# Forgetting attention and a gated feed-forward on one core: attention of the first two batches ahead of the load issues, score tiles paired across batches, the last project in two halves

## The chip, the cores and the metric

The kernel runs on one core of one Trainium2 chip. The metric is the time of one execution on the device, in microseconds (us); lower is better. Line numbers L… are those of the kernel before; the changed kernel's lines stand three to five further down.

## The reference

Attention with a decay, over 8 batches of 8 heads with 576 tokens and 64 values a head, then a feed-forward block with root-mean-square norm:

```python
scores = q @ k.T / 8 + (cum[i] - cum[j])        # cum = cumsum(log(clip(f)))
attn = softmax(where(j > i, -1e9, scores)); x = attn @ v          # tokens by (heads * 64)
xn = x / sqrt(mean(x * x) + 1e-6) * rms_g
out = (silu(xn @ w_gate) * (xn @ w_val)) @ w_out    # 4608 x 512 -> 1536 -> 512
```

## The kernel before

Tokens of a batch are cut into five blocks of 128 (the last has 64; `LAST` = 4). For each query block `qi` and key block, TensorE makes a score tile for all 8 heads at once in one of two `sc` tiles of PSUM (L468), ScalarE takes the exponent into one of eight `PT` tiles (L486), GpSimd zeroes the upper triangle of the diagonal tile (L493), and TensorE multiplies the tiles of a query block by `Vs` (L512), the values scaled with the decay (L443, by VectorE in the first two batches and by GpSimd later). VectorE divides by the sum (L526, L528) into `x`; ScalarE squares it (L544), GpSimd makes the root (L548, L549), ScalarE scales (L556), and the result is turned into `xT`: on TensorE for the first two groups (L564), by a transposing DMA later (L578).

The feed-forward works on nine groups of 512 tokens: one for each batch's first 512, and one (`xTr`) of the last 64 of all batches. A `gate` is a pair of matmul blocks (L623, `wg` and `wv`), a tanh on ScalarE (L635) and two products on VectorE (L637, L630) into `hT`. For group 0, and for group 1 in this setting, a gate takes 4 chunks of 128 tokens. A `project` is 12 matmuls with `wo` into one `ff` tile (L648), a copy into `ores` (L661) and a store (L665, L674). Four `ff` tiles in PSUM serve all of this. While group 0 runs, VectorE folds `rms_g` into the weights (`weigh`, L357), since group 0 takes it from `xT`.

The order on every engine comes from a planner (`Plan.run`), which runs when the program is built: each piece of work is a unit with an engine, an assumed duration, a key, units it depends on, and ring buffers it takes and gives. A clock steps through assumed times; an engine that is free takes the ready unit with the lowest key. What it writes down is a fixed order per engine; on the chip each engine works through its own list and waits at the head of it. `SEEDS` shift a few keys at random before this. Loads are units of the queue that issues them (SP, or GpSimd, which has the casting loads of q, k, v and the weights), with keys from -20 to -9.25 for batch 0 and the weights; the attention of the first two batches has keys from -9 upwards. Later batches have keys by group.

In the last project the 512 columns of one `ff` tile are copied in two halves, by ScalarE and by VectorE, and stored by SP and ScalarE, 64 rows each.

Of the kernel before, what the change touches and what calls it, by code (L numbers as in the profile page):

```python
# [13 lines left out]
ACT = mybir.ActivationFunctionType  # L14
# [2 lines left out]


XPE, DT1, WIDE1 = 2, 0, 0
SEEDS = (84657, 89789, 467802, 542893, 578548, 39129, 244901, 271533, 218637, 949787, 548179, 128631, 931054,  # L20
         308866, 728294, 159527, 419945, 172881, 127940, 429679, 253611, 69364, 46042, 834979, 30072, 763446,
         468225, 737993, 973909, 205828, 651373, 635195, 93425, 157523, 690164, 692741, 943081, 404019, 832688)


class Unit:
# [14 lines left out]
class Plan:  # L40
# [114 lines left out]
def fox_ffn_kernel(ctx, tc, q, k, v, f, moe_w_gate, moe_w_val, moe_w_out, moe_rms_g, out):  # L155
    nc = tc.nc
    B, H, S, D = q.shape
# [56 lines left out]
    def pe(dur, key, emit, deps=(), take=(), give=()):  # L214
        return P.add("PE", dur, key, emit, deps, take, give, lat=0.2)
# [179 lines left out]
    def turn(b, j, key):  # L395
        p0, n = rows(j)
        for dst, nm in ((T_QT, "q"), (T_KT, "k")):
            def emit(dst=dst, nm=nm):
                nc.sync.dma_start_transpose(out=dst[hold_QT[b].slot][:, :, p0:p0 + n],
                                            in_=T_qk[hold_qk[b, nm, j].slot][0:n, :])  # L400
            turned[b, nm, j] = load("SP", 1.3, (16 * n, 0.00029), key, emit, [qkload[b, nm, j]],
                                    take=[hold_QT[b]], give=[hold_qk[b, nm, j]], late=1.8)

    def turn_pe(b, j, two, key):
# [130 lines left out]
    def norm(b, js, key):  # L535

        n = rows(js[0])[1]
        sq, ms, rs = (s[0:n, b, js[0]:js[-1] + 1] for s in stat)
        us = []
        for i, j in enumerate(js):  # L540
            hx = hold_x[b, j]

            def emit(i=i, hx=hx):
                nc.scalar.activation(junk[0:n, :], T_x[hx.slot][0:n, :], ACT.Square, accum_out=sq[:, i:i + 1])  # L544
            us.append(act(0.73, key, emit, [evac[b, j, 0], evac[b, j, 1]]))

        def emit():
            nc.gpsimd.tensor_scalar(ms, in0=sq, scalar1=1.0 / DM, op0=ALU.mult, scalar2=1e-6, op1=ALU.add)  # L548
            nc.gpsimd.tensor_tensor(rs, ms, mhalf[0:n, 0:len(js)], ALU.pow)  # L549
        r = pool(0.9, key, emit, us + [iden_f])  # L550
        for i, j in enumerate(js):
            hx, hn = hold_x[b, j], Hold("xn", 1)
            g, c = (b, j * 128) if j < LAST else (B, b * 64)

            def emit(i=i, n=n, hx=hx, hn=hn):
                nc.scalar.mul(T_xn[hn.slot][0:n, :], T_x[hx.slot][0:n, :], rs[:, i:i + 1])  # L556
            u = act(0.72, key - 0.02, emit, [r], take=[hn], give=[hx])
            if g < XPE:
                hf = Hold("ff", 1)

                def tr(hn=hn, hf=hf):
                    tp = T_ff[hf.slot].bitcast(BF16)
                    for dc in range(NDC):
                        nc.tensor.transpose(tp[:, dc * 128:(dc + 1) * 128], T_xn[hn.slot][:, dc * 128:(dc + 1) * 128],  # L564
                                            ident)
                t = pe(0.25, key, tr, [u, iden], take=[hf], give=[hn])

                def cp(hf=hf, g=g, c=c):
                    tp = T_ff[hf.slot].bitcast(BF16)[:, 0:512].rearrange("p (c t) -> p c t", t=128)
                    to = T_of[g][hold_xT[g].slot][:, :, c:c + 128]  # L570
                    if g == 0:
                        nc.vector.tensor_tensor(to, tp, bcast(rgT, 128), ALU.mult)
                    else:
                        nc.vector.tensor_copy(to, tp)
                pieces[b, j] = dve(0.69 if g == 0 else 0.42, key - 0.02, cp, [t, c_rg], take=[hold_xT[g]], give=[hf])
            else:
                def tr(n=n, hn=hn, g=g, c=c):
                    nc.sync.dma_start_transpose(out=T_of[g][hold_xT[g].slot][:, :, c:c + n],  # L578
                                                in_=T_xn[hn.slot][0:n, :])
                pieces[b, j] = load("SP", 1.3, (16 * n, 0.00029), key, tr, [u], take=[hold_xT[g]], give=[hn])  # L580


    order = [(b, qi) for b in range(2) for qi in range(LAST)] + [(0, LAST), (1, LAST)]
# [2 lines left out]

    def qkey(b, qi, ahead=0.0):
        if b < 2:
            return (2 * b - 9 + 0.2 * (START[qi] + ahead)) if qi < LAST else 0.3 + 0.6 * b + 0.04 * ahead
        return akey(b, (START[qi] + ahead) / 13)  # L590

    todo = []
    for b, qi in order:
        if b >= 2 or qi == LAST or (b == 1 and qi >= 4 - 2 * DT1):
            turn(b, qi, qkey(b, qi) - 0.25)
        elif (b, qi) in {(0, 0), (0, 1), (0, 3), (1, 0), (1, 2)}:
            turn_pe(b, qi, (b, qi) in {(0, 1), (1, 0), (1, 2)}, qkey(b, qi) - 0.25)
# [12 lines left out]

    hold_hT = [Hold("hT", 4) for _ in range(G)]
# [28 lines left out]
        return dve(0.69, key - 0.1, last, [a, uv], take=[hold_hT[g]], give=[ha, hv])  # L640

    def project(g, j, key):
        hf, ho = Hold("ff", 1), Hold("ores", 1)
        last = None
        for part in range(3):
            def emit(part=part):
                for fc in range(part * 4, part * 4 + 4):
                    nc.tensor.matmul(T_ff[hf.slot], lhsT=T_hT[hold_hT[g].slot][:, fc, j * 128:(j + 1) * 128],  # L648
                                     rhs=wo[:, fc, :], start=(fc == 0), stop=(fc == NFC - 1))
            deps = [last] if part else []  # L650
            deps += hdone[g, j, part]
            deps += Lo[part // 2:part // 2 + 1 + part % 2]
            last = pe(0.865, key + 0.0001 * part, emit, deps, take=[hf] if part == 0 else [],
                      give=[hold_hT[g]] if part == 2 else [])
        end = g == B and j == 3
        halves = (slice(0, 256), slice(256, 512)) if end else (slice(0, 512),)
        hf.n = len(halves)
        cs = []
        for add, copy, cols in zip((act, dve), (nc.scalar.copy, nc.vector.tensor_copy), halves):
            cs.append(add(0.59 if len(halves) == 1 else 0.36, key - 0.05,  # L660
                          lambda copy=copy, cols=cols: copy(T_ores[ho.slot][:, cols], T_ff[hf.slot][:, cols]),  # L661
                          [last], take=[ho], give=[hf]))
        if g < B:
            t0 = g * S + j * 128
            load("SP", 0.4, (128, 0.0055), key, lambda: nc.sync.dma_start(out=out[t0:t0 + 128, :], in_=T_ores[ho.slot]), cs,  # L665
                 give=[ho])
            return
        ho.n = 2
        for i in range(2):
            eng, queue = ("ACT", nc.scalar) if end and i else ("SP", nc.sync)  # L670

            def st(i=i, queue=queue):
                t0 = (2 * j + i) * S + LAST * 128
                queue.dma_start(out=out[t0:t0 + 64, :], in_=T_ores[ho.slot][i * 64:(i + 1) * 64, :])  # L674
            load(eng, 0.4, (64, 0.0055), key, st, cs, give=[ho])
# [65 lines left out]
```

## Time and profile before

| | us |
|---|---|
| median of 3 runs | 386.04 |
| lowest and highest | 382.62, 386.28 |
| the profiled execution | 384.47 |
| its span, first to last instruction | 382.6 |

In the profile PE is TensorE's matmuls and PEld its weight loads, DVE is VectorE, ACT ScalarE, POOL GpSimd, SP SyncE; SPq, ACTq and POOLq are their queues, where DMAs are issued. A row of a timeline has its start, its length, the engine, the line, the operation with output and input tiles, a count, and in brackets how long the engine had been idle and what ended that. A row of the stretches has, for each engine, busy time and instructions in the stretch.

### The profile page before, as it was taken

How to read it: one execution, taken by the hardware profiler on the slowest of the kernel's cores; microseconds unless marked ns; L12 is line 12 of the kernel's file. 1: busy time of each engine (PE TensorE's matmuls, PEld its weight loads, DVE VectorE, ACT ScalarE, POOL GpSimd, SP SyncE). 2: the span in 40 equal slices, each digit the busy share in tenths (PEclk: the TensorE clock that was granted, in tenths of full speed). 3: DMA queues.
4: the chain of work that ended last, by engine and by line, in shares of the span. 5: the costliest groups of instructions: out<-in, count | busy, mean ns of one | idle time of the engine just before them, and what ended most of it. 6: DMA issues, size and time to landing. Idle time of an engine off the chain costs nothing.

```text
span 382.6 us, 9657 instructions
## 1 busy us (share of the span) xinstructions
PE 357.8 (94%) x3896; PEld 214.3 (56%) x3942; DVE 219.4 (57%) x458; ACT 237.5 (62%) x378; POOL 201.0 (53%) x280
## 2 busy tenths in 40 slices
PE   1799898989998999999999999999999999999994
PEld 1589875779964555555555555555555544444441
DVE  5567999556654647455655465545654645555430
ACT  5685637978988656947695669656966442332321
POOL 8975699499998665975497549841302000000000
PEclk9999999999999999999999999999999999999999
DMA  9999999979999999994999789972120210100004
GB/s 141 200 217 204 217 171 153 159 176 151 135 127 162 133 124 152 165 150 81 132 154 174 88 114 160 178 97 56 36 57 29 55 34 29 55 25 32 28 29 110
DMA packets 128869, 44.84 MB, mean 117 GB/s; under 512 B 117300, under 2 KB 121912, under 8 KB 128824
## 3 DMA queue, kind: packets, MB, share of 16 engines
q0 software_dynamic: 76368, 23.34, 61.8%
q1 hardware_dynamic: 52376, 20.74, 29.1%
q8 instruction: 31, 0.51, 0.6%
q10 hardware_dynamic: 80, 0.13, 0.2%
q14 instruction: 14, 0.11, 0.1%
HBM read 37.90 MB, written 9.44 MB: 124 GB/s over the span
## 4 chain that ended last, share of the span: by engine, by line
PE 73%; POOL 8%; DVE 7%; DMA 6%; issue 3%; ACT 1%; POOLq 0%; ACTq 0%; DVEq 0%
PE ff L623 40%; PE ff L648 22%; PE ff L512 6%; PE sc L468 5%; DMA wv<-in_moe_w_val_dram 3%; DMA xT<-xn 3%; POOL qk L315 2%; POOL Vs L443 2%; DVE hT L630 1%; POOL v L338 1%; DVE wv L357 1%; DVE ga L637 1%; ACT xn L556 1%; DVE Vs L443 1%; POOL PT L493 1%
## 5 line engine op out<-in xcount | busy, mean ns | idle before, releaser
L637 DVE SCALAR_TENSOR_TENSOR ga<-th,ff 128x512 f32<-128x512 f32 x108 | 73.4, 684 | 81.7 <-ACT th L635 80.4
L635 ACT ACTIVATE th<-ff 128x512 f32<-128x512 f32 x108 | 63.8, 595 | 75.2 <-PE ff L623 58.8
L648 PE MATMUL ff<-wo,hT 128*128 128x512 bf16 x410 | 104.9, 379 | 1.1 <-DVE x L528 0.2
L486 ACT ACTIVATE PT<-sc 128x1024 bf16<-128x1024 f32 x96 | 94.8, 1016 | 11.6 <-PE sc L468 11.5
L623 PE MATMUL ff<-xT,wg 128*128 128x128 bf16 (+1 forms) x658 | 96.1, 286 | 3.9 <-DMA xT<-xn 1.7
L623 PE MATMUL ff<-xT,wv 128*128 128x128 bf16 (+1 forms) x663 | 97.1, 286 | 2.4 <-DVE hT L630 1.7
L630 DVE SCALAR_TENSOR_TENSOR hT<-ga,ff 128x512 bf16<-128x512 f32 x108 | 73.0, 685 | 21.8 <-PE ff L623 18.7
L623 PEld LDWEIGHTS <-wg 128*128 128x128 bf16 x720 | 53.6, 98 | 39.2 <-issue 3.3
L623 PEld LDWEIGHTS <-wv 128*128 128x128 bf16 x720 | 53.2, 98 | 37.9 <-issue 2.6
L648 PEld LDWEIGHTS <-hT 128*128 128x128 bf16 x432 | 40.6, 98 | 46.4 <-issue 0.5
L493 POOL TENSOR_SCALAR_AFFINE_SELECT PT<-PT 128x1024 bf16<-128x1024 bf16 x32 | 35.3, 1104 | 48.3 <-ACT PT L486 48.3
L512 PEld LDWEIGHTS <-PT 128*128 128x128 bf16 x896 | 38.4, 99 | 15.0 <-POOL PT L493 2.3
L512 PE MATMUL ff<-Vs,PT 128*128 128x65 bf16 x896 | 43.5, 197 | 1.7 <-POOL PT L493 1.5
L443 POOL TENSOR_TENSOR Vs<-v,decT 128x512 bf16<-128x512 f32 (+1 forms) x30 | 31.5, 1049 | 17.3 <-DMA v<-in_v_dram 16.2
L661 ACT COPY ores<-ff 128x512 f32<-128x512 f32 (+1 forms) x36 | 20.8, 578 | 27.6 <-PE ff L648 27.6
L338 POOL DMA_DIRECT2D v<-in_v_dram x39 | 35.6, 915 | 3.4 <-DMA v<-in_v_dram 2.0
L468 PE MATMUL sc<-QT,KT 64*128 64x128 bf16 (+1 forms) x960 | 34.3, 214 | 1.6 <-ACT PT L486 1.3
L528 DVE TENSOR_TENSOR x<-ff,rden 128x256 f32<-128x256 f32 (+1 forms) x80 | 33.8, 423 | 2.8
L526 DVE RECIPROCAL rden<-ff 128x4 f32<-128x4 f32 (+1 forms) x80 | 14.1, 177 | 33.7 <-PE ff L512 33.5
L468 PEld LDWEIGHTS <-KT 64*128 64x128 bf16 x960 | 24.9, 97 | 13.7 <-issue 10.8
L556 ACT ACTIVATE xn<-x,rs 128x512 bf16<-128x512 f32 (+1 forms) x40 | 27.3, 716 | 7.0 <-POOL rs L549 4.4
L315 POOL DMA_DIRECT2D qk<-in_q_dram x34 | 30.0, 886 | 1.2 <-POOLq L725 0.8
(63 smaller groups left out, 218.0 us busy)
## 6 DMA issues: line engine op xcount, KB each, us to landing
out_dram<-ores SPq DMA_DIRECT2D x32, 256.0 KB, 2.4
v<-in_v_dram POOLq DMA_DIRECT2D x31, 256.0 KB, 6.3
qk<-in_q_dram POOLq DMA_DIRECT2D x26, 128.0 KB, 4.8
qk<-in_k_dram POOLq DMA_DIRECT2D x26, 128.0 KB, 6.2
wv<-in_moe_w_val_dram POOLq DMA_DIRECT2D x3, 512.0 KB, 13.2
wg<-in_moe_w_gate_dram POOLq DMA_DIRECT2D x3, 512.0 KB, 11.5
wo<-in_moe_w_out_dram POOLq DMA_DIRECT2D x2, 768.0 KB, 16.4
v<-in_v_dram POOLq DMA_DIRECT2D x8, 128.0 KB, 6.7
```

What stands on the lines that cost most here:

```text
L315: nc.gpsimd.dma_start(out=T_qk[h.slot][0:n, :].rearrange("p (h d) -> p h d", d=D), in_=src[b, :, p0:p0 + n, :].rearrange("h p d -> p h d"))
L338: queue.dma_start(out=T_v32[h.slot][0:n, :, :], in_=v[b, :, p0:p0 + n, :].rearrange("h p d -> p h d"))
L443: eng.tensor_tensor(T_Vs[hv.slot][0:n, j, :, 0:D], T_v32[h.slot][0:n, :, :], bcast(dj, D), ALU.mult)
L468: nc.tensor.matmul(t[:, par, c:c + n], lhsT=kt[r, p, kj * 128:(kj + 1) * 128], rhs=qt[r, p, qi * 128:qi * 128 + n], start=True, stop=True)
L486: nc.scalar.activation(T_of_p[hp.slot][:, 0:2 * half].rearrange("p (a c) -> p a c", a=2)[:, :, 0:cols], T_sc[h.slot][:, :, 0:cols], ACT.Ex ...
L493: nc.gpsimd.affine_select(out=d, in_=d, pattern=[[0, 8], [1, n]], compare_op=ALU.is_ge, fill=0.0, base=0, channel_multiplier=-1)
L512: nc.tensor.matmul(po[:, p, :], lhsT=T_of_p[h.slot][:, c:c + 128], rhs=vs[:, kj, 2 * p + par, :], start=(kj == 0), stop=(kj == qi))
L623: nc.tensor.matmul(T_ff[h.slot][:, c:c + n], lhsT=w[:, dc, fc * 128:(fc + 1) * 128], rhs=xT[:, dc, t0:t0 + n], start=(dc == 0), stop=(dc = ...
L630: nc.vector.scalar_tensor_tensor(hT, in0=three[0], scalar=0.5, in1=three[1], op0=ALU.mult, op1=ALU.mult)
L635: th = act(0.6, key - 0.1, lambda: nc.scalar.activation(T_th[ht.slot], T_ff[hg.slot], ACT.Tanh, scale=0.5), [ug], take=[ht])
L637: a = dve(0.69, key - 0.1, lambda: nc.vector.scalar_tensor_tensor(T_ga[ha.slot], in0=T_th[ht.slot], scalar=1.0, in1=T_ff[hg.slot], op0=ALU ...
L648: nc.tensor.matmul(T_ff[hf.slot], lhsT=T_hT[hold_hT[g].slot][:, fc, j * 128:(j + 1) * 128], rhs=wo[:, fc, :], start=(fc == 0), stop=(fc == ...
```

## The change

Five things change in the code.

1. The attention of batches 0 and 1 gets keys from -18.8 (`BASE`) instead of -9, so it goes ahead of the weights' and later loads where an engine has both (GpSimd above all: masks and roots against load issues). Their values and norms follow their scores more closely (`VA` = 1 and `NA` = 1.2 instead of 2.5 and 3.5).
2. Score tiles are issued in pairs; the odd tile at the end of a batch, which stood alone, is now paired with the first tile of the next batch.
3. The last project makes its two halves of 256 columns one after the other, each with an `ff` and an `ores` tile of its own; both are copied by ScalarE, and there are four stores of 64 rows by 256 columns (three on SP, one on ScalarE) instead of two of 64 rows by 512.
4. The planner assumes a longer transposing DMA.
5. `SEEDS` are others.

```diff
-XPE, DT1, WIDE1 = 2, 0, 0
-SEEDS = (84657, 89789, 467802, 542893, 578548, 39129, 244901, 271533, 218637, 949787, 548179, 128631, 931054,
...
+BASE = -18.8
+VA, NA = 1, 1.2
+SEEDS = (579458, 693525, 233519, 938766, 177064, 479178, 872084, 34928, 716154, 894218, 4117, 601621, 491026,
...
-            turned[b, nm, j] = load("SP", 1.3, (16 * n, 0.00029), key, emit, [qkload[b, nm, j]],
+            turned[b, nm, j] = load("SP", 1.3, (16 * n, 0.00044), key, emit, [qkload[b, nm, j]],
...
-            return (2 * b - 9 + 0.2 * (START[qi] + ahead)) if qi < LAST else 0.3 + 0.6 * b + 0.04 * ahead
+            return (2 * b + BASE + 0.2 * (START[qi] + ahead)) if qi < LAST else 0.3 + 0.6 * b + 0.04 * ahead
...
-            if len(todo) == 2 or (b == 0 and kjs[-1] == qi) or kjs[-1] == LAST:
+            if len(todo) == 2 or (b == 0 and kjs[-1] == qi) or (b, kjs[-1]) == (B - 1, LAST):
...
-        values(b, qi, qkey(b, qi, qi + 2.5))
+        values(b, qi, qkey(b, qi, qi + (VA if b < 2 else 2.5)))
...
-            norm(b, js, qkey(b, js[-1], js[-1] + 3.5))
+            norm(b, js, qkey(b, js[-1], js[-1] + (NA if b < 2 else 3.5)))
...
+        ho, cs = [Hold("ores", 1) for _ in halves], []
+        for half, cols in enumerate(halves):
+            hf, last = Hold("ff", 1), None
+            for part in range(3):
...
+                        nc.tensor.matmul(T_ff[hf.slot][:, cols], lhsT=T_hT[hold_hT[g].slot][:, fc, j * 128:(j + 1) * 128],
+                                         rhs=wo[:, fc, cols], start=(fc == 0), stop=(fc == NFC - 1))
...
+            cs.append(act(0.36 if end else 0.59, key - 0.05, lambda hf=hf, cols=cols, half=half: nc.scalar.copy(
+                T_ores[ho[half].slot][:, cols], T_ff[hf.slot][:, cols]), [last], take=[ho[half]], give=[hf]))
...
+                eng, queue = ("ACT", nc.scalar) if half and i else ("SP", nc.sync)
...
+                    queue.dma_start(out=out[t0:t0 + 64, cols], in_=T_ores[ho[half].slot][i * 64:(i + 1) * 64, cols])
```

What this does to the order is seen at three places. The first is ScalarE in the head of the program, before: `KT` is the copy of turned keys, `hT` here the decay in a buffer that is free, `PT` an exponent tile, `junk` the square of `x0`, the first query block's result, `xn0` its scaled form.

```order
L282 ACTIVATE hT1_113<-hT1_113,mid_138 64x576
L427 COPY KT0_80<-ff0_123 128x4x128
L427 COPY KT0_80<-ff1_124 128x4x2x128
L486 ACTIVATE PT0_89<-sc0_121 128x1024
L486 ACTIVATE PT1_90<-sc0_121 128x1024
L486 ACTIVATE PT2_91<-sc1_122 128x1024
L427 COPY KT0_80<-ff0_123 128x4x128
L544 ACTIVATE junk_136,sq_139<-x0_99 128x512
L486 ACTIVATE PT3_92<-sc0_121 128x1024
L486 ACTIVATE PT4_93<-sc1_122 128x1024
L486 ACTIVATE PT5_94<-sc0_121 128x1024
L556 ACTIVATE xn0_105<-x0_99,rs_141 128x512
```

The same place of the changed kernel:

```order
L430 COPY KT0_80<-ff1_124 128x4x128
L285 ACTIVATE hT1_113<-hT1_113,mid_138 64x576
L489 ACTIVATE PT0_89<-sc0_121 128x1024
L430 COPY KT0_80<-ff1_124 128x4x2x128
L547 ACTIVATE junk_136,sq_139<-x0_99 128x512
L489 ACTIVATE PT1_90<-sc1_122 128x1024
L489 ACTIVATE PT2_91<-sc0_121 128x1024
L559 ACTIVATE xn0_105<-x0_99,rs_141 128x512
L489 ACTIVATE PT3_92<-sc1_122 128x1024
L489 ACTIVATE PT4_93<-sc0_121 128x1024
L489 ACTIVATE PT5_94<-sc1_122 128x1024
```

The first copy has moved ahead of the decay, the first exponent ahead of the second copy, the square of `x0` ahead of the exponents of the second query block, its scaling ahead of the third block's, and the third copy behind all of these.

The second place is VectorE while group 0 runs, before: `ga` and `hT0` are the two products of a gate, `wg` and `wv` the folding of `rms_g`, `Vs1` the scaling of batch 1's values.

```order
L637 SCALAR_TENSOR_TENSOR ga0_116<-th0_114,ff3_126 128x512
L357 TENSOR_SCALAR wg_127<-wg_127,rgT_130 128x512 x4
L443 TENSOR_TENSOR Vs1_88<-v322_85,decT_135 128x8x64
L444 CAST Vs1_88<-decT_135 128x8
L630 SCALAR_TENSOR_TENSOR hT0_112<-ga0_116,ff2_125 128x4x128
L637 SCALAR_TENSOR_TENSOR ga1_117<-th1_115,ff1_124 128x512
L357 TENSOR_SCALAR wv_128<-wv_128,rgT_130 128x512 x4
L630 SCALAR_TENSOR_TENSOR hT0_112<-ga1_117,ff3_126 128x4x128
```

The changed kernel, as many rows from the start of its list:

```order
L446 TENSOR_TENSOR Vs1_88<-v322_85,decT_135 128x8x64
L447 CAST Vs1_88<-decT_135 128x8
L430 COPY QT1_78<-ff1_124 128x4x2x128
L640 SCALAR_TENSOR_TENSOR ga1_117<-th0_114,ff0_123 128x512
L633 SCALAR_TENSOR_TENSOR hT0_112<-ga1_117,ff3_126 128x4x128
L575 TENSOR_TENSOR xT0_109<-ff0_123,rgT_130 128x4x128
L529 RECIPROCAL rden0_142<-ff3_126 128x4
L531 TENSOR_TENSOR x4_103<-ff3_126,rden0_142 128x4x64
L640 SCALAR_TENSOR_TENSOR ga1_117<-th1_115,ff1_124 128x512
```

The first results of batch 1 (`x4`) now stand between the gates of group 0, and the folding of the weights comes later in the list.

The third place is SP's list at the end, before, with the stores of the last group (two for each of its projects):

```order
L665 DMA out_0_dram<-ores1_119 128x512
L674 DMA out_0_dram<-ores2_120 64x512 x2
L674 DMA out_0_dram<-ores0_118 64x512 x2
L674 DMA out_0_dram<-ores1_119 64x512 x2
L674 DMA out_0_dram<-ores2_120 64x512
```

And changed:

```order
L666 DMA out_0_dram<-ores1_119 128x512
L676 DMA out_0_dram<-ores2_120 64x512 x2
L676 DMA out_0_dram<-ores0_118 64x512 x2
L676 DMA out_0_dram<-ores1_119 64x512 x2
L676 DMA out_0_dram<-ores2_120 64x256 x2
L676 DMA out_0_dram<-ores0_118 64x256
```

SP has two more stores behind those of the third project; one more store of the last project is on ScalarE's queue, as before.

More of the change, by code (lines that the diff above doesn't have):

```diff
@@ L19 @@
 XPE, DT1, WIDE1 = 2, 0, 0
-SEEDS = (84657, 89789, 467802, 542893, 578548, 39129, 244901, 271533, 218637, 949787, 548179, 128631, 931054,
-         308866, 728294, 159527, 419945, 172881, 127940, 429679, 253611, 69364, 46042, 834979, 30072, 763446,
-         468225, 737993, 973909, 205828, 651373, 635195, 93425, 157523, 690164, 692741, 943081, 404019, 832688)
+BASE = -18.8
+VA, NA = 1, 1.2
+SEEDS = (579458, 693525, 233519, 938766, 177064, 479178, 872084, 34928, 716154, 894218, 4117, 601621, 491026,
+         354719, 434034, 228013, 97395, 11681, 347647, 765825, 66081, 881721, 502518, 805631, 222054, 709678,
+         173299, 242848, 187611, 334030, 497482, 17147, 635799, 701044, 138540, 384064, 613012, 295955, 674079,
+         543307, 211343, 784335, 305669, 953268)
 class Unit:
@@ L579, in tr @@
                                                 in_=T_xn[hn.slot][0:n, :])
-                pieces[b, j] = load("SP", 1.3, (16 * n, 0.00029), key, tr, [u], take=[hold_xT[g]], give=[hn])
+                pieces[b, j] = load("SP", 1.3, (16 * n, 0.00044), key, tr, [u], take=[hold_xT[g]], give=[hn])
     order = [(b, qi) for b in range(2) for qi in range(LAST)] + [(0, LAST), (1, LAST)]
@@ L642, in project @@
     def project(g, j, key):
[L643 to L654, printed above, removed]
@@ L655, in project @@
         end = g == B and j == 3
         halves = (slice(0, 256), slice(256, 512)) if end else (slice(0, 512),)
[L657 to L662, printed above, removed]
+        ho, cs = [Hold("ores", 1) for _ in halves], []
@@ new lines, in project, with emit @@
+        for half, cols in enumerate(halves):
+            hf, last = Hold("ff", 1), None
+            for part in range(3):
+                def emit(part=part, hf=hf, cols=cols):
+                    for fc in range(part * 4, part * 4 + 4):
+                        nc.tensor.matmul(T_ff[hf.slot][:, cols], lhsT=T_hT[hold_hT[g].slot][:, fc, j * 128:(j + 1) * 128],
+                                         rhs=wo[:, fc, cols], start=(fc == 0), stop=(fc == NFC - 1))
+                deps = [last] if part else []
+                deps += hdone[g, j, part]
+                deps += Lo[part // 2:part // 2 + 1 + part % 2]
+                last = pe(0.865 / len(halves), key + 0.01 * half + 0.0001 * part, emit, deps,
+                          take=[hf] if part == 0 else [], give=[hold_hT[g]] if (part, cols.stop) == (2, 512) else [])
+            cs.append(act(0.36 if end else 0.59, key - 0.05, lambda hf=hf, cols=cols, half=half: nc.scalar.copy(
+                T_ores[ho[half].slot][:, cols], T_ff[hf.slot][:, cols]), [last], take=[ho[half]], give=[hf]))
@@ L663, in project, with st @@
         if g < B:
             t0 = g * S + j * 128
-            load("SP", 0.4, (128, 0.0055), key, lambda: nc.sync.dma_start(out=out[t0:t0 + 128, :], in_=T_ores[ho.slot]), cs,
-                 give=[ho])
+            load("SP", 0.4, (128, 0.0055), key, lambda: nc.sync.dma_start(out=out[t0:t0 + 128, :], in_=T_ores[ho[0].slot]),
+                 cs, give=ho)
             return
[L668 to L675, printed above, removed]
+        for half, cols in enumerate(halves):
+            ho[half].n = 2
+            for i in range(2):
+                eng, queue = ("ACT", nc.scalar) if half and i else ("SP", nc.sync)
+                def st(i=i, queue=queue, half=half, cols=cols):
+                    t0 = (2 * j + i) * S + LAST * 128
+                    queue.dma_start(out=out[t0:t0 + 64, cols], in_=T_ores[ho[half].slot][i * 64:(i + 1) * 64, cols])
+                load(eng, 0.4, (64, 0.0055 / len(halves)), key + 0.01 * half, st, [cs[half]], give=[ho[half]])
```

## The prediction

> **What bounds the kernel now.** I read the page first, then the stretches, then the waits of TensorE, and last the timeline at the head, around 40 to 82 us, and at the end. From the page, the engines' busy time:
>
> ```profile
> PE 357.8 (94%) x3896; PEld 214.3 (56%) x3942; DVE 219.4 (57%) x458; ACT 237.5 (62%) x378; POOL 201.0 (53%) x280
> ```
>
> TensorE is busy for 357.8 of 382.6 us, and nothing in the change takes a matmul away, so all that can be won lies in the 24.8 us in which it stands still. The stretches say where those are:
>
> ```profile
> 0.00:10.00 10.00, 2.13 (x25) 1.80 (x26) 4.93 (x24) 4.82 (x6) 8.80 (x17) 1.00 1.21 148
> 10.00:20.00 10.00, 7.18 (x95) 5.66 (x96) 5.94 (x16) 6.86 (x9) 9.05 (x11) 1.00 1.41 198
> ...
> 40.00:50.00 10.00, 8.98 (x167) 8.39 (x165) 10.00 (x23) 6.30 (x8) 6.97 (x9) 1.00 1.59 209
> 50.00:60.00 10.00, 9.47 (x131) 6.22 (x129) 9.93 (x23) 5.67 (x9) 9.79 (x11) 1.00 1.97 161
> ...
> 370.00:383.00 13.00, 7.63 (x35) 3.26 (x34) 0.42 (x1) 2.13 (x4) 0.00 (x0) 0.98 0.34 82
> ```
>
> The first figure behind the comma is TensorE's, then come PEld, DVE, ACT and POOL. TensorE loses 10.7 us in the first 20, 1.6 between 40 and 60, and 5.0 at the end (382.6 less 370, less 7.63). That is 17.3; the other 7.5 are spread over all the rest. Between 40 and 60 VectorE has no gap left (10.00 and 9.93). The waits of TensorE from 20 us on name the releasers:
>
> ```profile
> PE ff L623 <- DVE hT L630: 2.5, 3, 1.5
> PE ff L623 <- DMA xT<-xn: 1.7, 2, 1.3
> PE ff L512 <- POOL PT L493: 1.0, 1, 1.0
> PE ff L623 <- DVE ga L637: 0.5, 2, 0.3
> ```
>
> So the kernel is a TensorE stream with a head, a stretch where VectorE holds it back, and a tail. The change works on all three.
>
> **The head.** These rows carry the chain up to the sixth exponent:
>
> ```profile
> 6.98 0.78 ACT L282 ACTIVATE hT<-hT,mid 64x576 f32<-64x576 f32 x1 [0.27 <-DVE mid L275]
> 7.03 0.10 PEld L414 LDWEIGHTS <-qk 128*128 128x128 bf16 x1 [7.03 <-DMA qk<-in_k_dram]
> 7.74 1.01 PE L414 MATMUL ff<-ident,qk 128*128 128x128 bf16 x8 [7.74 <-DVE ident L263]
> 8.36 0.59 ACT L427 COPY KT<-ff 128x512 bf16<-128x512 bf16 x1 [0.61 <-PE ff L414]
> 10.79 1.06 PE L420 MATMUL ff<-ident,qk 128*64 128x128 bf16 x16
> 11.79 1.04 PE L468 MATMUL sc<-QT,KT 64*128 64x128 bf16 x16
> 11.90 1.31 ACT L427 COPY KT<-ff 128x1024 bf16<-128x1024 bf16 x1 [2.95 <-PE ff L420]
> 13.07 1.03 ACT L486 ACTIVATE PT<-sc 128x1024 bf16<-128x1024 f32 x1
> 14.79 1.94 ACT L486 ACTIVATE PT<-sc 128x1024 bf16<-128x1024 f32 x2 [0.70 <-PE sc L468]
> 17.75 0.63 ACT L544 ACTIVATE junk<-x 128x512 bf16<-128x512 f32 x1 [0.54 <-DVE x L528]
> 18.38 2.83 ACT L486 ACTIVATE PT<-sc 128x1024 bf16<-128x1024 f32 x3
> 21.12 0.72 ACT L556 ACTIVATE xn<-x,rs 128x512 bf16<-128x512 f32 x1
> 25.99 0.62 PE L468 MATMUL sc<-QT,KT 64*128 64x128 bf16 x16
> ...
> L528 DVE TENSOR_TENSOR x<-ff,rden 128x256 f32<-128x256 f32 (+1 forms) x80 | 33.8, 423 | 2.8
> ```
>
> In the changed order the identity is made before the second pair of load issues, so the first transposes start when their keys land, at 7.03. Their copy follows 0.62 later (8.36 less 7.74) and ends at 8.24; the first score tile, half of the 1.04, is done by 8.9. ScalarE does the decay's exponent (0.78) in the meantime, and the first exponent starts near 9.1 instead of 13.07: a lead of 4.0 us. I do not think it lasts. The keys of the second query block still need their two groups of transposes (some 1.06 each), which now stand behind the decay's transposes; I put their end at 12.4 against 11.85, and the 1.31 copy at 13.8 against 13.2. Then ScalarE's list has the square of `x0` ahead of the next exponents. For that VectorE must first make its own copy (as long as ScalarE's, to about 13.3) and then `x0` in two halves (0.42 each and a smaller reciprocal: about 1.2), so 14.5. Before, an exponent starts 0.63 behind the square's start; so the next one comes at 15.2, 0.4 later than the 14.79 of before. From there six places run on: two exponents (1.94), the scaling of `x0` (0.72), three exponents (2.83), to 20.7. Before, ScalarE has all of this and one 0.59 copy more done at 21.84 (21.12 and 0.72); with that copy the changed list is at 21.3. I give the 0.5 to handovers, since the third block's score tiles wait for one of two `sc` tiles to be read, and call the head level: 0.0, between -3.0 (three quarters of the lead kept) and +2.0 (two exponents' time lost at the square and the scaling that now stand in front of them).
>
> GpSimd's load issues of the fourth block and of most weights now stand behind the first mask, and some behind the first root, on an engine that is busy for 8.80 and 9.05 of 10 us already. I cost that at nothing, since the first gate comes only behind the sixth score tile; if that cover is gone, it falls under the +2.0.
>
> **The VectorE stretch.** Three rows of the timeline:
>
> ```profile
> 44.56 1.95 PE L623 MATMUL ff<-xT,wg 128*128 128x128 bf16 x32 [0.78 <-DVE hT L630]
> 62.84 0.47 PE L512 MATMUL ff<-Vs,PT 128*128 128x65 bf16 x10 [1.00 <-POOL PT L493]
> 81.66 1.05 PE L623 MATMUL ff<-xT,wv 128*128 128x128 bf16 x16 [1.46 <-DVE hT L630]
> ```
>
> Before, gates of group 0 follow each other and each wants two products from VectorE, while the folding and the scaling of values also sit there. Changed, batch 1's scores and values lie between them: TensorE has work that does not wait for a product. Of the 3.0 us of waits for `hT` and `ga`, the 1.5 that are not the wait at 81.66 should go; for the 1.46 at 81.66 and the mask's 1.00 I take half, since neither the order nor the trace says which wait is next there. That is 1.5 + 0.7 + 0.5, -2.7, of which I keep -2.5 as later waits will be a little longer; the ends are 0 (they only move) and -4.0 (all go). The closer values and norms (`VA`, `NA`) carry the risk here: a value block sooner behind its scores is a value block sooner at a mask; that is the second rival.
>
> **The pairs.** A block of score matmuls starts late by a little, since it follows blocks that use all rows:
>
> ```profile
> 171.72 1.03 PE L648 MATMUL ff<-wo,hT 128*128 128x512 bf16 x4
> 172.59 1.03 PE L623 MATMUL ff<-xT,wv 128*128 128x512 bf16 x4
> 173.55 0.64 PE L468 MATMUL sc<-QT,KT 64*128 64x64 bf16 x32
> ```
>
> Starts lie 0.87 apart between two blocks of four, and 0.96 ahead of the scores: 0.09 for each entry. Three pairs across batches save three entries: -0.3. The paired tile now waits for the next batch's turned keys. No row shows such a wait; the loads run far ahead, and I take nothing, with up to 1.3 (the longest wait for a transposing DMA) as the upper end.
>
> **The tail.**
>
> ```profile
> 367.16 10.52 PE L648 MATMUL ff<-wo,hT 128*128 128x512 bf16 x47
> 376.90 0.59 ACT L661 COPY ores<-ff 128x512 f32<-128x512 f32 x1 [3.77 <-PE ff L648]
> 377.76 0.37 ACT L661 COPY ores<-ff 128x256 f32<-128x256 f32 x1 [0.28 <-PE ff L648]
> 378.17 0.42 DVE L661 COPY ores<-ff 128x256 f32<-128x256 f32 x1 [10.02 <-ACT ores L661]
> 378.62 0.58 ACTq L674 DMA_DIRECT2D out_dram<-ores  x1
> ...
> 377.51 1.75 SPq L674 DMA_DIRECT2D out_dram<-ores  x3
> ...
> out_dram<-ores SPq DMA_DIRECT2D x32, 256.0 KB, 2.4
> out_dram<-ores SPq DMA_DIRECT2D x7, 128.0 KB, 2.3
> ```
>
> TensorE ends at 377.68, and VectorE's half of the copy waits for ScalarE's: the last copy ends at 378.59, the last issues at 379.20 and 379.26. Changed, TensorE does the same columns (24 matmuls of half the width), so I keep its end. The last copy then ends at 378.13, 0.46 sooner. But SP now has five stores behind the third project, whose copy ends 0.9 earlier (12 half matmuls and four more, some 1.75, lie behind it instead of 0.86), at 376.60. Five issues of 0.58 from there end at 379.5, 0.3 later than the 379.26 of before. SP's queue takes the place of the copy. A store a quarter of 256 KB lands perhaps 0.05 sooner by the two sizes above. Tail: +0.2, between -0.5 (the copy's gain whole) and +0.6. [...]
>
> **Sum.** 0.0 - 2.5 - 0.3 + 0.2 = -2.6 against the profiled execution's 384.47 (span 382.6 and 1.9 around it), that is 381.9, so 382. The profiled run lies 1.6 below the median of the three, 386.04, and 1.9 over the lowest. What a measurement can tell from no change is about 1%, 3.8 us.
>
> **Rivals.**
>
> *The head keeps its lead.* If the square of `x0` is not late (VectorE's 1.31 copy done sooner) the exponents go on from 9.1 nearly without a gap, and 3 of the 4.0 us stay, with 0.5 from faster matmuls there: 382.0 - 3.5 = 378.5. For it: ScalarE is idle for 5.2 of the first 10 us and 3.1 of the next. Against it: the second block's copies follow loads that are issued behind the identity now, and transposes behind the decay's. The score rows show a slow state that could end: 16 matmuls take 1.04 at 11.79 and 0.62 at 25.99, with the granted clock recorded as 1.00 from 10 to 20. [...] Chance 0.27.
>
> *Masks take the place of products (slower).* In batches 0 and 1 eight value blocks have a mask from GpSimd, which is busy for nine tenths of the first 20 us and most of 50 to 60 with load issues; a value block with a smaller key stands sooner at its mask. One such wait is in the profile, 1.00 at 62.84. If seven more come at 1.0 each, 382.0 + 7 = 389.0. It decides from the third on, which eats the forecast gain; five or more make it slower than before by over half a per cent. For it: the waits row of masks. Against it: values behind the gates have other work ahead of them. Chance 0.15.
>
> *VectorE stays the bound.* Its work is the same but for one copy, and part of what it loses is not order. The lengths of the foldings:
>
> ```profile
> L357 DVE TENSOR_SCALAR wg<-wg,rgT x12: 334/337/722, 41.6 to 65.0; 128x512 bf16<-128x512 bf16 x12
> L357 DVE TENSOR_SCALAR wv<-wv,rgT x12: 334/344/1555, 45.0 to 67.0; 128x512 bf16<-128x512 bf16 x12
> ```
>
> (shortest, median, longest in ns.) The longest takes 1.2 us more than the median, while GpSimd is at work beside it. If that stays, the waits only move: 384.5 - 0.3 + 0.2 = 384.4, no change. [...] Chance 0.18.
>
> **Chances and range.** The forecast has 0.40, with a range of its own from 379.5 to 384.5; a quarter of it lies below 380.6, the bound of 1%. With the first rival (0.26 of its 0.27) that makes faster 0.36; the second rival gives slower 0.15; the rest, 0.49, is no change. Lows of all terms (-3.0, -4.0, -0.3, -0.5) would give 376.7, highs (+2.0, 0, +1.0, +0.6) 388.1. The range 377 to 387 leaves out most of the second rival and a little below.
>
> **What would show it.** Right: the first exponent near 9 us and the sixth's end near 21; no wait over 0.5 of TensorE for `hT` between 40 and 60; five SP issues in a row at the end, the last 1.8 or 1.9 behind the last matmul. Wrong: the first gate on TensorE before 19 us (first rival), several waits of L512 for masks of about 1.0 (second), a VectorE stretch full for 20 us with the same waits for `hT` (third), or a loss after 120 us, for which nothing here speaks.

## The result and the profile after

| | kernel before | changed kernel |
|---|---|---|
| median of 20 runs each, us | 382.96 | 382.76 |
| lowest and highest, us | 381.74, 388.22 | 381.31, 389.49 |
| ratio to before, 95% interval | | 0.9995 (0.9974 to 1.0015) |
| the profiled execution, us | 384.47 | 382.43 |
| its span, us | 382.6 | 380.7 |

No change that can be measured. The two profiles lie 2.0 us apart, but that of before is 1.5 above its own median, so a difference between the two pages is not yet one between the kernels.

Page and waits of TensorE of the changed kernel, from 20 us on (us in total, times, longest):

```profile
PE 357.7 (94%) x3906; PEld 214.8 (56%) x3954; DVE 219.1 (58%) x457; ACT 236.8 (62%) x379; POOL 201.0 (53%) x280
...
PE ff L515 <- DVE ga L640: 1.6, 2, 1.4
PE sc L471 <- DMA KT<-qk: 0.8, 1, 0.8
PE ff L423 <- DMA qk<-in_k_dram: 0.7, 2, 0.4
PE ff L567 <- ACT xn L559: 0.6, 1, 0.6
PE ff L423 <- DMA qk<-in_q_dram: 0.5, 1, 0.5
```

The waits for `hT` (2.5 before) are gone but for 0.2. Value blocks (L515) wait for VectorE in their place, and transposes and scores for loads of q and k, which no row of before showed. The timeline has the places:

```profile
8.44 1.02 ACT L489 ACTIVATE PT<-sc 128x1024 bf16<-128x1024 f32 x1
11.76 1.30 ACT L430 COPY KT<-ff 128x1024 bf16<-128x1024 bf16 x1 [2.29 <-PE ff L423]
13.37 0.63 ACT L547 ACTIVATE junk<-x 128x512 bf16<-128x512 f32 x1 [0.31 <-DVE x L531]
...
19.40 1.02 ACT L489 ACTIVATE PT<-sc 128x1024 bf16<-128x1024 f32 x1 [0.97 <-PE sc L471]
...
19.30 1.89 PE L626 MATMUL ff<-xT,wg 128*128 128x128 bf16 x16
...
57.33 3.21 DVE L360 TENSOR_SCALAR wg<-wg,rgT 128x512 bf16<-128x512 bf16 x4
60.47 1.26 DVE L640 SCALAR_TENSOR_TENSOR ga<-th,ff 128x512 f32<-128x512 f32 x2
...
61.18 0.65 PE L515 MATMUL ff<-Vs,PT 128*128 128x65 bf16 x16 [1.38 <-DVE ga L640]
...
72.52 0.29 PE L471 MATMUL sc<-QT,KT 64*128 64x64 bf16 x8
73.58 0.40 PE L471 MATMUL sc<-QT,KT 64*128 64x128 bf16 x8 [0.77 <-DMA KT<-qk]
```

The longest wait, 1.38 at 61.18, ends with the first of VectorE's products at 60.47, which gives an `ff` tile back; ahead of it stand four foldings that took 3.21 us instead of the 1.3 that four of the shortest (0.333) would take. The 0.77 at 73.58 is the pair: the odd tile of a batch (64x64) is done, and the next batch's tile, now in the same block, waits for its keys.

The end of the program:

```profile
365.63 10.55 PE L655 MATMUL ff<-wo,hT 128*128 128x512 bf16 x59
370.76 7.41 SPq L676 DMA_DIRECT2D out_dram<-ores  x9
376.27 0.37 ACT L662 COPY ores<-ff 128x256 f32<-128x256 f32 x1 [0.89 <-PE ff L655]
376.67 0.56 ACTq L676 DMA_DIRECT2D out_dram<-ores  x1
...
out_dram<-ores SPq DMA_DIRECT2D x3, 64.0 KB, 2.0
```

TensorE ends at 376.18, SP's last issue at 378.17, 1.99 behind it (before: 379.26 less 377.68, 1.58), and the span 4.52 behind it (before: 382.6 less 377.68, 4.92).

### The profile page after: what moved, and what is told of

It reads as the page before. It is cut to its first block, busy times and chain, and to the rows that moved or that the text cites. A ratio compares the mean times of both kernels' runs of the same rounds, so it can differ in the third digit from the quotient of the medians.

```text
span 380.7 us, 9668 instructions
## 1 busy us (share of the span) xinstructions
PE 357.7 (94%) x3906; PEld 214.8 (56%) x3954; DVE 219.1 (58%) x457; ACT 236.8 (62%) x379; POOL 201.0 (53%) x280
## 4 chain that ended last, share of the span: by engine, by line
PE 76%; DMA 14%; POOL 4%; issue 2%; ACT 2%; DVE 1%; SPq 0%; ACTq 0%; POOLq 0%
PE ff L626 41%; PE ff L655 23%; PE ff L515 6%; PE sc L471 5%; DMA wo<-in_moe_w_out_dram 4%; DMA qk<-in_q_dram 4%; DMA qk<-in_k_dram 3%; DMA KT<-qk 2%; POOL qk L318 2%; POOL PT L496 1%; DMA out_dram<-ores 1%; POOL v L341 0%; ACT PT L489 0%; DVE x L531 0%; ACT junk L547 0%
## 5 line engine op out<-in xcount | busy, mean ns | idle before, releaser
L655 PE MATMUL ff<-wo,hT 128*128 128x512 bf16 (+1 forms) x423 | 106.6, 373 | 1.1 <-issue 0.2
L515 PEld LDWEIGHTS <-PT 128*128 128x128 bf16 x896 | 38.0, 98 | 16.0 <-issue 2.0
L515 PE MATMUL ff<-Vs,PT 128*128 128x65 bf16 x896 | 42.8, 195 | 2.3 <-DVE ga L640 1.6
L341 POOL DMA_DIRECT2D v<-in_v_dram x39 | 34.3, 883 | 6.2 <-DVE rden L529 3.5
L547 ACT ACTIVATE junk<-x 128x512 bf16<-128x512 f32 (+1 forms) x40 | 25.1, 627 | 8.5 <-DVE x L531 8.1
```

The costliest lines, as they stand in the source:

```text
L341: queue.dma_start(out=T_v32[h.slot][0:n, :, :], in_=v[b, :, p0:p0 + n, :].rearrange("h p d -> p h d"))
L515: nc.tensor.matmul(po[:, p, :], lhsT=T_of_p[h.slot][:, c:c + 128], rhs=vs[:, kj, 2 * p + par, :], start=(kj == 0), stop=(kj == qi))
L655: nc.tensor.matmul(T_ff[hf.slot][:, cols], lhsT=T_hT[hold_hT[g].slot][:, fc, j * 128:(j + 1) * 128], rhs=wo[:, fc, cols], start=(fc == 0), ...
```

## The experiments

All times are ratios to the kernel before, run beside each on the same chip, with 95% intervals; 0.1% is 0.38 us.

**1. The tail alone.** The kernel before with the changed `project`; everything ahead of it stands in the same order.

```diff
         halves = (slice(0, 256), slice(256, 512)) if end else (slice(0, 512),)
+        ho, cs = [Hold("ores", 1) for _ in halves], []
...
```

> The kernel before with the last project of the changed kernel (halves in banks and tiles of their own, four stores of 64 rows by 256 columns) and nothing else; all that stands ahead of it is in the same order. By the prediction's step (five issues in a row on SP's queue take the place of the copy) the end moves by +0.2 us: the last issue on SP ends 1.9 behind the last matmul instead of 1.6, and the span ends 5.1 to 5.2 behind it instead of 4.9. The rival is read from the profile after: the smaller stores land sooner than the later issue costs, so the span ends 4.5 behind the last matmul and the time falls by 0.4.

Measured: 0.9986 (0.9963 to 1.0009). Its span and the rows of its end:

```profile
core 0 of [0], span 379.4 us
...
364.32 10.55 PE L652 MATMUL ff<-wo,hT 128*128 128x512 bf16 x60
...
369.44 7.40 SPq L673 DMA_DIRECT2D out_dram<-ores  x9
```

SP ends 1.97 behind the last matmul (376.84 less 374.87), as forecast, but the span ends 4.53 behind it: 0.39 sooner than before. The time alone could not say this; the rows do, and they are those of the changed kernel. The prediction's issue was right and its landing too long.

This profile has a second use. Its order is that of before up to the last project, yet TensorE's waits differ:

```profile
PE ff L623 <- DVE hT L630: 0.8, 2, 0.6
```

The wait of 1.46 at 81.66 and that of 1.28 at 116.58, which stand in the profile of before, are not in this one. They belonged to an execution, not to the order.

**2. Is VectorE on the path?** The folding on 8 of 512 columns, the other 504 left out, in both kernels.

```diff
-                    nc.vector.tensor_scalar_mul(w[:, dc, c0:c1], w[:, dc, c0:c1], rgT[:, dc:dc + 1])
+                    nc.vector.tensor_scalar_mul(w[:, dc, c0:c0 + 8], w[:, dc, c0:c0 + 8], rgT[:, dc:dc + 1])
```

> The changed kernel with the folding of rms_g done on 8 of 512 columns of each weight chunk; the other 504 are left out (the order on every engine is the same, VectorE has some 7 us less to do between 40 and 75 us). If VectorE still bounds the stretch from 40 to 80, the 2.0 us that TensorE waits for ga go and little takes their place: 1.5 to 3 us faster. If the late loads of q and k bound it (TensorE waits 2.8 us for DMAs from 24 to 75), those waits stay or grow by what is won: less than 0.7 us faster.

> The kernel before with the folding of rms_g done on 8 of 512 columns, the other 504 left out, the order the same. Both theories have VectorE's products as the waits of before, so both expect a gain: the 3.0 us of waits for hT and ga, of which the one at 81.66 may stay: 1.5 to 3 us faster. If it is under 0.5 us, VectorE's load was not what the stretch of before hung on, and the step of the prediction that sizes this stretch fell with it.

Measured: changed kernel 0.9907 (0.9874 to 0.9939), kernel before 0.9992 (0.9960 to 1.0024). The first is what the VectorE theory says, 3.4 us below the changed kernel's own 0.9995, though VectorE lost only 3.8 us of work there (11.7 us for 24 foldings, then 7.9; the forecast had some 7). The second is a miss for both theories: VectorE lost 5.1 us of work (11.3, then 6.2) and no time came of it. So the old order kept the foldings off the path, and the new one puts them on it. What each costs, shortest, median and longest in ns, in the changed kernel as it is (first pair) and the sums and means with 8 columns (second pair):

```profile
L360 DVE TENSOR_SCALAR wg<-wg,rgT x12: 333/340/2101, 46.3 to 70.7; 128x512 bf16<-128x512 bf16 x12
L360 DVE TENSOR_SCALAR wv<-wv,rgT x12: 333/341/1279, 63.9 to 74.0; 128x512 bf16<-128x512 bf16 x12
```

```profile
L360 DVE TENSOR_SCALAR wg<-wg,rgT 128x8 bf16<-128x8 bf16 x12 | 4.4, 433 | 0.0
L360 DVE TENSOR_SCALAR wv<-wv,rgT 128x8 bf16<-128x8 bf16 x12 | 3.5, 423 | 0.0
```

Cut to a 64th of the columns, a folding still takes 0.43 us on average, and in the kernel before one of these lasts 1.99 (the shortest 0.21): the long ones are not long from their own work.

**3. Are the late loads on the path?** The changed kernel with a sixth of the output weights loaded.

```diff
-                    out=wo[:, i * 6:(i + 1) * 6, :],
-                    in_=moe_w_out[i * 768:(i + 1) * 768, :].rearrange("(c p) f -> p c f", p=128))
+                    out=wo[:, i * 6:i * 6 + 1, :],
+                    in_=moe_w_out[i * 768:i * 768 + 128, :].rearrange("(c p) f -> p c f", p=128))
...
-                                         rhs=wo[:, fc, cols], start=(fc == 0), stop=(fc == NFC - 1))
+                                         rhs=wo[:, fc // 6 * 6, cols], start=(fc == 0), stop=(fc == NFC - 1))
```

> The changed kernel with a sixth of the output weights loaded: each of the two loads brings 128 rows of 768, and the project uses these rows six times (the other rows are left out; the order on every engine is the same, the DMA engines move 2.6 MB less between 32 and 50 us). If late loads of q and k bound the stretch from 24 to 75, TensorE's 2.8 us of waits for DMAs shrink to under 1 and the time falls by 1.5 to 2.5 us. If VectorE bounds it, the waits move to ga and hT and the time stays within 0.7 us.

Measured: 0.9970 (0.9929 to 1.0010). The waits of its TensorE:

```profile
PE ff L515 <- DVE ga L640: 3.0, 2, 1.8
...
PE ff L423 <- DMA qk<-in_k_dram: 0.9, 1, 0.9
```

This lies between the two forecasts (1.5 to 2.5 us, or within 0.7). Some 1 us may come from the lighter load, but the interval holds no gain too. The waits for DMAs fell from 2.7 us in the rows of the changed kernel to 1.9, and the wait for `ga` grew from 1.6 to 3.0: its longest, 1.8, is the one at 61.18, here at 59.24. So the loads bound at most a smaller part of the stretch.

**4. Put the foldings elsewhere.** If they are in the way between 46 and 75, move them: behind group 1's gates in VectorE's list (group 1 then takes `rms_g` from its `xT`, like group 0), or to ScalarE. In the first diff `fold` holds the six foldings and `prod` a gate's two products.

```diff
-                    if g == 0:
+                    if g < 2:
                         nc.vector.tensor_tensor(to, tp, bcast(rgT, 128), ALU.mult)
...
+        order = [u for u in P.run() if u not in fold.values()]
+        for (nm, i), u in fold.items():
+            at = max(order.index(p[nm == "v"]) for g in range(2) for p in prod[g, i])
+            order.insert(at + 1, u)
```

> The changed kernel with the six foldings of rms_g moved in VectorE's list behind the last gates of group 1 that read the same chunk (some 85 to 115 us, where VectorE is busy half the time); group 1's four copies of the turned xn multiply by rms_g as group 0's do (0.69 us planned instead of 0.42). All else stands in the same order. If in the new order the foldings lie on TensorE's path between 40 and 75, as the 3.2 us between the kernel with 8 columns and the changed kernel's own median of 20 runs say, moving them gives most of that back: 1.5 to 3 us faster than the kernel before. If leaving them out only helped because VectorE had less work in all, the waits appear again between 85 and 120 and the time stays within 0.7 us of the kernel before.

> The same move of the foldings in the kernel before, with its own order otherwise. Without the foldings that kernel was 0.3 us faster, inside the interval. If its stretch hangs on something other than the foldings (loads, the head), the move gives nothing: within 1 us of the kernel before. If the result with 8 columns was an accident of the runs, this gains 1.5 us or more like the changed kernel.

Measured: 1.0108 (1.0058 to 1.0157) and 1.0217 (1.0172 to 1.0261). Both theories miss: it is slower in both orders. The profile of the first is of its slowest execution, 3.4 us above the median of six. The changed kernel with late foldings, VectorE first, then GpSimd at the same time, then the value block that waited:

```profile
96.94 5.90 DVE L360 TENSOR_SCALAR wv<-wv,rgT 128x512 bf16<-128x512 bf16 x4
...
97.47 1.11 POOL L497 TENSOR_SCALAR_AFFINE_SELECT PT<-PT 128x1024 bf16<-128x1024 bf16 x1
98.53 1.05 POOL L447 TENSOR_TENSOR Vs<-v,decT 128x512 bf16<-128x512 f32 x1
...
101.63 1.06 POOL L447 TENSOR_TENSOR Vs<-v,decT 64x512 bf16<-64x512 f32 x1
...
103.45 1.04 PE L516 MATMUL ff<-Vs,PT 128*128 128x65 bf16 x16 [3.59 <-DVE x L532]
...
L360 DVE TENSOR_SCALAR wv<-wv,rgT x12: 334/691/3943, 82.8 to 117.5; 128x512 bf16<-128x512 bf16 x12
```

GpSimd computes without a gap from 97.47 to 102.9, and VectorE's four foldings end with it; one of them took 3.94 us instead of 0.33. GpSimd's own operations keep their 1.05. In the kernel before, with late foldings too, VectorE is busy for 9.86 of the 10 us from 95 to 105 and GpSimd for 4.99 of the first 5, and a value block that waits for VectorE comes 3.27 late, at 103.28. So the place with a half idle VectorE is a bad one. GpSimd, which is not idle there, may be the reason; no run took its work away. How much of the loss is group 1's longer copies was not separated.

On ScalarE, at the same places of the plan:

```diff
-                    nc.vector.tensor_scalar_mul(w[:, dc, c0:c1], w[:, dc, c0:c1], rgT[:, dc:dc + 1])
+                    (nc.scalar.mul if w is wv else nc.vector.tensor_scalar_mul)(
+                        w[:, dc, c0:c1], w[:, dc, c0:c1], rgT[:, dc:dc + 1])
```

> The changed kernel with the 12 foldings of the value weights (wv) done by ScalarE at the same places of the plan; those of wg stay on VectorE, the order is otherwise the same. VectorE loses 5.6 us of 11.7 (mean 527 ns each, against a shortest of 333), ScalarE gets 12 at some 0.5 us between 62 and 76, where it is busy 13.2 of 20 us. If VectorE's foldings are on TensorE's path in the new order, and longer beside GpSimd's work: 0.8 to 2.5 us faster than the changed kernel. If ScalarE's tanh and exponents become late instead: no change or up to 2 us slower.

> The changed kernel with all 24 foldings done by ScalarE, at the same places. VectorE loses 11.7 us between 46 and 75; ScalarE gets some 12 us there and would be busy about 38 of 40 us from 40 to 80. If VectorE is the bound and ScalarE has room: 2 to 3 us faster than the changed kernel, like the one with 8 columns. If ScalarE takes VectorE's place: TensorE's waits read th, xn and PT of ScalarE, and the time is 0 to 3 us over the changed kernel.

Measured: 1.0098 (1.0062 to 1.0135) and 1.0248 (1.0215 to 1.0281). Both are slower than the forecasts allowed (up to 2 and up to 3 us over the changed kernel; measured 3.9 and 9.7). ScalarE needs 0.71 us for one on average, and 0.72 with all of them there. In that kernel it is busy for 39.5 of the 40 us from 40 to 80. VectorE's waits from 40 to 82 us and a piece of the chain that ended last (start, length, work) read:

```profile
DVE ga L640 <- ACT th L638: 17.9, 5, 6.5
...
58.47 2.45 ACT wg L360 x4
61.43 0.70 DVE ga L640
62.17 0.64 PE ff L515 x16
```

VectorE has time now and waits 17.9 us for tanh, which stands behind the foldings in ScalarE's list: the bound has moved one engine on, as the rival had it, at over three times its highest price. No version tried here beats the kernels and computes the same.

**5. What the edits are worth without shifts.** `SEEDS` empty in both kernels; then the kernel before without shifts with the new keys of attention (-18.8), and with the closer values and norms too.

```diff
-SEEDS = (84657, 89789, 467802, ...
+SEEDS = ()
...
-            return (2 * b - 9 + 0.2 * (START[qi] + ahead)) if qi < LAST else 0.3 + 0.6 * b + 0.04 * ahead
+            return (2 * b - 18.8 + 0.2 * (START[qi] + ahead)) if qi < LAST else 0.3 + 0.6 * b + 0.04 * ahead
```

> The kernel before with its table of random shifts empty: the planner's keys alone set the order. If the shifts matter, 1 to 4 us slower than the kernel before; if they are noise, within 1 us.

> The changed kernel with its table of random shifts empty. Beside the kernel before without shifts it shows what the new keys, pairs and tail are worth without tuning. If attention ahead of the loads is good in itself, it is 1 to 3 us under that kernel; if the new shifts repair what the new keys do, it is 1 us or more over it; if both are noise, within 1 us.

> The kernel before without shifts (389.31 us) with one number changed: the attention of the first two batches gets the changed kernel's keys (-18.8 for -9), so that it goes ahead of load issues; values, norms, pairs and the last project are as before. In the kernel before without shifts TensorE waits 5.4 us for GpSimd's masks, which stand behind load issues; in the changed kernel without shifts (385.26) no such wait is left. If the keys do that by themselves: 3 to 4 us faster than without, some 385.5 to 386.5, with mask waits under 1.5 us. If the closer values and norms, the pairs and the tail bring it: within 1 us of 389.3.

> As the kernel with the keys of attention alone, and the values and norms of the first two batches set closer too (1 and 1.2 for 2.5 and 3.5). What is left to the changed kernel without shifts are the pairs, the last project and one planner constant. If pairs and tail are worth what the prediction's lower ends say (0.3 and 0.4): 385.5 to 386.5. If the closer values stand at masks, as the prediction's second rival has it, it is slower than with the keys of attention alone by 1 us or more.

| | ratio to the kernel before | TensorE's waits for masks, us |
|---|---|---|
| before, with its shifts | 1 | 1.5 |
| before, no shifts | 1.0156 (1.0109 to 1.0203) | 5.4 |
| the same, new keys of attention | 1.0128 (1.0095 to 1.0160) | 3.0 |
| the same, closer values and norms | 1.0084 (1.0047 to 1.0121) | none |
| changed, no shifts (pairs, tail and planner's constant too) | 1.0059 (1.0025 to 1.0093) | none |
| changed, with its shifts | 0.9995 (0.9974 to 1.0015) | 0.5 |

The rows on which the second column rests, of the kernel before without shifts and, in the second fence, of the one with new keys of attention:

```profile
PE ff L510 <- POOL PT L491: 5.4, 4, 2.7
...
24.20 0.73 PE L510 MATMUL ff<-Vs,PT 128*128 128x65 bf16 x10 [2.70 <-POOL PT L491]
```

```profile
PE ff L510 <- POOL PT L491: 2.3, 2, 1.5
...
PE ff L510 <- POOL P L491: 0.7, 1, 0.7
```

Without shifts the change is worth 0.97% (3.7 us), more than the 1 to 3 that were forecast, and the intervals of the two kernels without shifts are apart. Single steps, 0.3 to 0.4% each, are inside their intervals; the new keys alone bring 0.3%, 1.1 us, where the two sides expected 3 to 4 or under 1. The masks' column, from one profile each, shows the order of the steps. But the shifts of before had taken 1.56% by themselves (6.0 us, for 1 to 4 forecast), part of it from the same waits, and those of the changed kernel find 0.64%. Both end at the same time.

## Why the prediction was right, and where it was not

The time, the range and the largest chance (no change) came out. The sum of -2.6 was made against the profiled 384.47, which lies 1.5 above the median of 20 runs; against the medians the change is -0.2, and most of the sum is wrong. That 382 came so near is luck: a base 1.5 too high and a sum 2.4 too low. The 24.8 us in which TensorE was read as standing still were too many as well: that trace holds 3896 of 3942 matmuls. The first experiment's holds all of its own, and there TensorE stands still for 19.2 us (379.4 less 360.2), with no gap from 120 to 300.

**The head, 0.0: right.** The first exponent starts at 8.44 (forecast: near 9), the sixth ends at 20.4 (near 21), the first gate starts at 19.30, and the lead is lost at the places named, the second keys and the square of `x0`. In experiments 1 to 3, whose records are whole, TensorE's idle time in the first 40 us is 11.2 and 11.6 in the old order and 10.6 and 10.7 in the new: 0.75 us more work there. At the start the 16 matmuls of a gate take 1.89 us (at 19.30), later 1.07; by this pace the 0.75 are worth an estimated 0.4.

**The VectorE stretch, -2.5: this step failed.** It took the waits for `hT` and half of the waits at 81.66 and 62.84 as won. The first went as forecast, and the mask's wait too, but the sum of waits between 40 and 80 did not fall: 4.4 us in the changed kernel's rows, 3.2 in those of the first experiment, whose order there is that of before, and 2.9 in those of before. Two things were wrong. The wait at 81.66 was priced as a property of the order, and it was one of that execution. And the step took TensorE's new work between the gates as work that needs no product. A value block takes an `ff` tile, though, and the one at 61.18 gets it only when VectorE's product of a gate has read it (again in experiment 3, 1.78 at 59.24). So the foldings, off the path before, came to lie on it (3.4 us by the second experiment). That is the third rival, *VectorE stays the bound*, nearly to its price (384.4 against 384.47); the forecast gave it 0.18. It came in another form than its sign said, with waits for `ga` and not for `hT`; VectorE is busy for 36.4 of the 40 us from 40 to 80 (34.5 before). Why a folding gets long, no run shows. In the fourth experiment one lasted 3.94 us (the shortest 0.33), beside several of GpSimd's instructions of some 1.05.

**The pairs, -0.3 and nothing for the keys:** not run alone. The wait that the step could not size is there at 73.58 with 0.77, and with 1.04 in the profile with late foldings; in those of the changed order in experiments 2 and 3 it is not. Between +0.7 and -0.3.

**The tail, +0.2: the sign was wrong,** -0.4 in both profiles that have it. The issues cost what was forecast: the last ends 0.4 later behind the last matmul. The term that was mis-sized is what comes behind it, 0.05 shorter by the forecast: from SP's last issue to the end of the span it is 2.5 us (380.7 less 378.17) in place of 3.3 (382.6 less 379.26). The median landings, 2.0 us for 64 KB against 2.3 for 128 KB, are 0.3 of these 0.8. The semaphore events of the two traces give SP's last store itself: it lands 2.02 us after its issue began, and 2.70 in the kernel before, where ScalarE's last store was issued 0.09 us ahead of it. That is 0.7; 0.1 lies behind the landing. Whether two stores at once make the 2.70 was not tried.

The parts, -0.4 for the head, +1.2 for the stretch, -0.3 for the pairs and -0.4 for the tail, make +0.1 beside a measured -0.2 (the pair's wait of 0.77 is in the +1.2). They are read from one or two profiles each, and the waits of one order differ by some tenths between profiles, so this agreement proves little.

**The rivals.** The head kept no lead. The 0.5 from faster matmuls in this rival is in no run: with late foldings eight score matmuls take 0.40 at 15.18, against 0.61 at 15.06 in the changed kernel, but the first gate starts at 19.00 there, within the 18.96 to 19.42 of the six profiles with this order of the head. Masks did not take the place of products: the closer values, in which the forecast saw the risk, go with fewer waits for masks (3.0 us, then none, in the table above); why is open.

## What to carry to other kernels

Here the tuned order of the old kernel held much of what the better rule brings. Compare a structural edit with the tuning off on both sides, and expect less than the difference when it is on. Price a wait only if it stands in several executions of the same order. Before giving an engine's free time to a piece of work, look at what the other engines do then: here the foldings in a half idle VectorE, beside a computing GpSimd, were worse than in a full one (1.0108 against 0.9995).

## What the runs showed of the hardware

**In some profiles TensorE's clock is halved after a wait.** With the value weights folded on ScalarE, a wait of 1.79 us ends at 59.97. The stretches there (TensorE's busy time first, the granted clock third from the end):

```profile
58.00:60.00 2.00, 0.21 (x6) 0.09 (x3) 2.00 (x5) 1.54 (x2) 2.00 (x3) 1.00 2.09 181
60.00:62.00 2.00, 2.00 (x41) 1.82 (x41) 1.62 (x4) 0.60 (x1) 1.11 (x3) 0.55 1.68 220
62.00:64.00 2.00, 2.00 (x37) 1.87 (x37) 1.20 (x3) 1.06 (x3) 1.59 (x3) 0.60 1.60 166
64.00:66.00 2.00, 2.00 (x57) 1.48 (x50) 0.00 (x0) 2.00 (x4) 1.64 (x2) 1.00 1.93 74
```

By the two shares of 0.55 and 0.60 the clock is at half for 3.4 us, in which an estimated 1.7 us are lost on top of the wait. In stretches of half a us the clock reads 0.50 for 3.4 us also after a wait of 1.92 us that ends at 75.34 (closer values and norms without shifts) and after two of 0.75 and 0.65 that end at 68.15 and 69.45 (new keys without shifts); in the late foldings it does so for 6.8 us, from within the wait of 3.59. It reads 1.00 after the 2.26 us of the kernel with all foldings on ScalarE:

```profile
62.17 0.64 PE L515 MATMUL ff<-Vs,PT 128*128 128x65 bf16 x16 [2.26 <-DVE ga L640]
...
62.00:64.00 2.00, 1.80 (x48) 1.71 (x48) 1.93 (x7) 2.00 (x3) 0.67 (x1) 1.00 1.70 221
```

So length alone does not decide, and what does was not shown.

**The slow start ends at different times.** Gates of 16 matmuls take 1.89 at 19.30 and 1.07 at 24.25 in the changed kernel. In others (all foldings on ScalarE; then new keys without shifts):

```profile
20.49 1.06 PE L626 MATMUL ff<-xT,wv 128*128 128x128 bf16 x16
```

```profile
25.80 1.90 PE L621 MATMUL ff<-xT,wv 128*128 128x128 bf16 x16
```

Full pace comes at about 20 us in the one and after 27.7 in the other, where waits of 1.53 and 1.81 lie in the first 24 us; the granted clock reads 1.00 all that while. These are two orders. The changed kernel and its five variants with shifts have the same order in the head, and there the first gate's second block, 16 matmuls with `wv`, takes 1.06 us in three profiles (at 20.49, 20.76 and 21.02) and 1.63, 1.81 and 1.77 in the others (at 21.40, 21.07 and 21.53). Of a us at the slow pace, 0.43 is lost where TensorE has work (1.89 for 1.07). How much of the spread between the runs of one kernel this and the halvings make was not separated.
